# Part of attention's set-up moved behind its first row passes, and more dummy matmuls ahead of the experts

## The chip, the core and the metric

The kernel is one program on one core of a Trainium2 chip. The metric is the device time of one execution, in microseconds, and lower is better.

## The reference

Sliding-window attention with sink tokens, a top-1 mixture of eight experts, and a dense layer pair, one after the other on 1536 tokens:

```
keep = (pos_k < n_sink) | ((pos_q >= pos_k) & (pos_q - pos_k < window))     # 2 batches, 8 heads, 768 tokens, 64 wide
a = exp(where(keep, q @ k.T / 8, -1e9) - rowmax); a /= a.sum + 1e-9
x = (a @ v), heads side by side                                              # 1536 x 512
xn = x / (|x| + 1e-6);  en = expert_emb / (|expert_emb| + 1e-6)
logits = xn @ en.T / tau;  e = argmax;  gate = softmax(logits)[e]
out[t] = gate[t] * (relu(x[t] @ w1[e[t]]) @ w2[e[t]])                        # 512 -> 1024 -> 512
h = out @ w_in;  return max(0.01 * h, h) @ w_out                             # 512 -> 2048 -> 512
```

## The kernel before, in words

Three stages share TensorE. **Attention** runs over 96 items (batch, group of four heads, block of 128 queries, head). An item is a product sc of q with the keys near the block, a row pass on VectorE (line 266: adds a mask of the kind m0, m1, ma, mb or mc, and takes the row's extreme), an exponential on ScalarE (line 268), a transpose of the probabilities and a product with v. Before that, `turns` transposes q and k: TensorE writes tk or tq (line 196), ScalarE copies the high half (lines 202, 216) and VectorE subtracts out the low half, head_k and head_q (lines 207, 217), since float32 products are made of rounded pairs. Blocks 0 to 2 of a group are turned by the functions in the list `first`, blocks 3 to 5 by those in `second`, at steps given by the table SECOND. The masks are made in `setup`, before all this, on VectorE (`penal`, line 116).

**The router** reads each finished block of x. Its set-up (`router_setup`) is a generator of which one piece is issued a step from step 16 on: first the norm of the eight expert embeddings (`norm`, lines 680 to 686, on 8 x 1 elements), their scaling (lines 606 to 608) and transposes, then small tables. At the end of attention a last product rk ranks the tokens, `id_list` makes the list ids of token numbers for each expert by twelve small products (ipa), and GpSimd gathers rows of x by it.

**The experts** follow in a fixed order of widths. Weights come in slots of 512 KB (slot_raw, line 997, on SyncE's DMA queue); ScalarE copies a slot's rounded high half (line 1001) and VectorE subtracts out its low half (line 1002). The first expert here is 128 wide (`moe_narrow`). It uses slots 0 to 7, the second expert slots 8 to 15: TensorE turns the gathered rows (tr), ScalarE and VectorE make mxT of them; then four times twelve products hp with slot 0, 2, 4 or 6, a relu hr on ScalarE (line 1222), two transposes th, the halves h on ScalarE and VectorE (lines 1230, 1231), and six products acc with slot 1, 3, 5 or 7. The second expert's rows become slot_big (line 1073). TensorE's instructions are issued in the order in which the code is written; those of the other engines are ordered by the Tile scheduler, which uses simulated times, and each engine then works through its own list.

`stir(c, n)` issues n matmuls of zeros, 128 x 512, whose result is not read. Two such groups stand around the products ipa, with the counts in WARM: their operand hot is a tile that GpSimd clears after attention. Attention has a group of seven of its own at the program's start, on the tile warm.

Of the kernel before, what the change touches and what calls it, by code (L numbers as in the profile page):

```python
# [7 lines left out]
F32 = mybir.dt.float32  # L8
F32R = mybir.dt.float32r
BF16 = mybir.dt.bfloat16  # L10
# [4 lines left out]
AF = mybir.ActivationFunctionType  # L15
# [6 lines left out]
P = 128  # L22
# [26 lines left out]
MAN = set()  # L49
STIR = {}  # L50
FIRST = [11, 13, 15, 17, 19, 21]
SECOND = [1, 2, 3, 4, 5, 6]
# [29 lines left out]
def setup(c):  # L82
# [37 lines left out]
    nc.vector.tensor_tensor(out=first[:, 1, :], in0=keep[:, P:2 * P], in1=sink[:, 0, :], op=ALU.max)  # L120
    c.m0 = mp.tile([P, P], F32, name="m0")
    penal(c.m0, first[:, 1, :])
    c.m1 = mp.tile([P, 2 * P], F32, name="m1")
    penal(c.m1[:, 0:P], first[:, 0, :])
    penal(c.m1[:, P:2 * P], keep[:, P:2 * P])
    c.ma = mp.tile([P, 2 * P + SINK], F32, name="ma")
    penal(c.ma[:, 0:2 * P], keep)
    penal(c.ma[:, 2 * P:], sink[:, 0, 0:SINK])
    c.mb = mp.tile([P, 2 * P + SINK], F32, name="mb")
    penal(c.mb[:, 0:P], keep[:, 0:P])  # L130
    penal(c.mb[:, P:P + SINK], sink[:, 0, 0:SINK])
    penal(c.mb[:, P + SINK:], keep[:, P:2 * P])
    c.mc = mp.tile([P, 2 * P + SINK], F32, name="mc")
    penal(c.mc[:, 0:SINK], sink[:, 0, 0:SINK])
    penal(c.mc[:, SINK:], keep)
    c.los = cp.tile([P, B * H * QB], F32, name="los")


def attention(c, ctx):
# [45 lines left out]
    def turns(b, pr):  # L185
# [28 lines left out]
        def q_part(c0, j):  # L214
            t, w, qt = turn(rq[:, :, j], c0, f"q{j}"), slice(c0 * P, (c0 + 3) * P), two[j][1]
            nc.scalar.activation(out=qt[:, 0, w], in_=t, func=AF.Copy, scale=-0.125)  # L216
            later(step[0] >= 0, lambda: nc.vector.scalar_tensor_tensor(
                out=qt[:, 1, w], in0=t, scalar=-0.125, in1=qt[:, 0, w].bitcast(F32), op0=ALU.mult, op1=ALU.subtract))

# [11 lines left out]
    load_qk(0, 1, 0, 3)  # L231
    c.warm = att.tile([P, 512], BF16, tag="warm", name="warm", bufs=1)
    nc.vector.memset(c.warm, 0.0)
# [16 lines left out]
    def score(b, g, i, h):  # L250
        if h == 0:
            u = units[b, g, i] = Ctx()
            u.p = wk.tile([P, 4, W3], F32, tag="p", name=f"p{b}{g}{i}", bufs=PB)
            u.pt = {}
        u = units[b, g, i]
        off, n, m, _, s0 = SPAN[i]
        kt, qt = heads[b, 4 * g + h]
        sc = psc.tile([P, W3], F32, tag="sc", name=f"sc{b}{g}{i}{h}")
        w = max(n, 2 * P)
        for half in range(2):  # L260
            nc.tensor.matmul(sc[:, 0:w], lhsT=qt[:, half, i * P:(i + 1) * P], rhs=kt[:, off:off + w],  # L261
                             start=half == 0, stop=half == 1)
        p = u.p[:, h, 0:n]
        col = ((b * 2 + g) * QB + i) * 4 + h
        lo = c.los[:, col:col + 1]
        nc.vector.tensor_tensor_reduce(out=p, in0=sc[:, 0:n], in1=m, scale=1.0, scalar=3.0e38,  # L266
                                       op0=ALU.add, op1=ALU.min, accum_out=lo)
        later(1, lambda: nc.scalar.activation(out=p, in_=p, func=AF.Exp, scale=-1.0, bias=lo))  # L268
        if h == 3 and i >= 2:
            u.sp = wk.tile([P, 4, SINK], F32, tag="sp", name=f"sp{b}{g}{i}")  # L270
            later(2, lambda: nc.gpsimd.tensor_copy(u.sp, u.p[:, :, s0:s0 + SINK]))
# [70 lines left out]
    first, second = group_turns(0, 0)  # L342
    setting = router_setup(c, ctx)
    stir(7)
    n = len(items)
    for _ in range(2):
        first.pop(0)()
    s = 0
    while s < n or after:
# [5 lines left out]
        if s < n:  # L355
# [5 lines left out]
            at = 4 * j + h  # L361
            if s < 3:
                for _ in range(2):
                    if first:
                        first.pop(0)()
            if at in SECOND:
                second.pop(0)()
            if k + 1 < len(groups):
# [11 lines left out]
                if at == 23:  # L380
                    assert not first and not second
                    second = then
            score(b, g, i, h)
        if 0 <= s - LAG1 < n:
            flip(*items[s - LAG1])
        if s >= 16:
            next(setting, None)
        if 0 <= s - LAGS < n and items[s - LAGS][3] == 3 and items[s - LAGS][2] >= 2:
# [204 lines left out]

def router_setup(c, ctx):


# [18 lines left out]

    yield
    c.tri = cp.tile([P, P], BF16, name="tri")
# [13 lines left out]
    c.qsel = table("qsel", NB, 1, -OUT)  # L631
    yield
    c.low = cp.tile([P, E, E], F32, name="lowtri")
# [5 lines left out]
    for n in range(E):  # L639
        nc.gpsimd.memset(c.cb[:, 0, n:n + 1], float(WIDTH[n]))  # L640
        nc.gpsimd.memset(c.cb[:, 1, n:n + 1], float(BASE[n]))
        nc.gpsimd.memset(c.ordv[:, n:n + 1], float(ORDER[n]))
    yield
    c.ss = cp.tile([P, NTT], F32, name="ss")
# [619 lines left out]

WARM = [3, 8]


def stir(c, n):

    if n:  # L1270
        t = c.pacc.tile([P, 512], F32, tag="acc", name=f"stir{c.uid()}")
        for _ in range(n):
            c.nc.tensor.matmul(t, lhsT=c.hot[:, 0:P], rhs=c.hot, start=True, stop=True)

# [187 lines left out]
def program(tc, q, k, v, n_sink, window, emb, tau, w1, w2, w_in, w_out, out):  # L1462
# [11 lines left out]
    with ExitStack() as ctx:  # L1474
# [11 lines left out]
        with tc.manual_schedule(engines={PE}), ExitStack() as mctx:  # L1486
            c.mo = mctx.enter_context(tc.tile_pool(name="m_wk", bufs=1))
            c.conv = [mctx.enter_context(tc.tile_pool(name=f"conv{i}", bufs=1)) for i in range(CONV)]
            c.yT = c.mo.tile([P, 4, YW], F32, name="yT")
            c.hot = c.mo.tile([P, 512], BF16, tag="y", name="hot", bufs=3)  # L1490
            c.nc.gpsimd.memset(c.hot, 0.0)
            for kk in range(4):
# [37 lines left out]
```

## Time and profile before

| what | value |
|---|---|
| median of three runs | 621.79 us (618.84 to 622.26) |
| the profiled execution, its own time | 618.77 us |
| its span, first to last instruction | 617.0 us |
| TensorE matmul busy | 588.9 us, 95% of the span |
| VectorE, ScalarE, GpSimd busy | 396.6, 292.9, 55.1 us |
| mean granted clock of TensorE | 0.971 of full |

The span leaves out 1.8 us around the first and the last instruction. A busy share is an average over stages with different limits, so the stretches of the next sections say more than the table. The granted clock has two levels, 0.50 (1.2 GHz) and 1.00 (2.4 GHz); a value between them is a mean over a stretch.

### The profile page before, as it was taken

How to read it: one execution, taken by the hardware profiler on the slowest of the kernel's cores; microseconds unless marked ns; L12 is line 12 of the kernel's file. 1: busy time of each engine (PE TensorE's matmuls, PEld its weight loads, DVE VectorE, ACT ScalarE, POOL GpSimd, SP SyncE). 2: the span in 40 equal slices, each digit the busy share in tenths (PEclk: the TensorE clock that was granted, in tenths of full speed). 3: DMA queues.
4: the chain of work that ended last, by engine and by line, in shares of the span. 5: the costliest groups of instructions: out<-in, count | busy, mean ns of one | idle time of the engine just before them, and what ended most of it. 6: DMA issues, size and time to landing. Idle time of an engine off the chain costs nothing.

```text
span 617.0 us, 10038 instructions
## 1 busy us (share of the span) xinstructions
PE 588.9 (95%) x3603; PEld 537.8 (87%) x3604; DVE 396.6 (64%) x953; ACT 292.9 (47%) x556; POOL 55.1 (9%) x156
## 2 busy tenths in 40 slices
PE   7899999997699999999999999799999999999996
PEld 4799999895599998889989998698998998899894
DVE  7889788856699659997973799953224322242230
ACT  4777787755687444524652463442223322332230
POOL 3011013003122010001000000010000100020001
PEclk7899999996699999999999999999999999999999
DMA  5777560013998683379499600000000100010001
GB/s 119 172 162 173 144 167 2 2 68 110 346 359 302 196 315 106 119 248 372 157 343 338 240 0 2 0 35 18 1 1 0 52 2 0 1 52 0 1 1 56
DMA packets 87994, 73.71 MB, mean 119 GB/s; under 512 B 54024, under 2 KB 70408, under 8 KB 87936
## 3 DMA queue, kind: packets, MB, share of 16 engines
q1 hardware_dynamic: 85824, 66.22, 34.4%
q0 software_dynamic: 2112, 6.75, 3.1%
q8 instruction: 31, 0.51, 0.4%
q14 instruction: 27, 0.22, 0.1%
HBM read 66.67 MB, written 6.29 MB: 118 GB/s over the span
## 4 chain that ended last, share of the span: by engine, by line
PE 87%; DVE 6%; DMA 2%; issue 2%; ACT 1%; SPq 1%; POOL 0%; POOLq 0%; DVEq 0%
PE acc L1079 30%; PE hp L1079 30%; PE xp L298 6%; PE sc L261 4%; PE hp L1176 3%; PE acc L1188 3%; PE tp L280 3%; DMA slot_raw<-in_moe_w 2%; PE tq L196 1%; PE lg L716 1%; PE xp L301 1%; PE tr L1068 1%; PE xTp L697 1%; PE tk L196 1%; DVE slot L1054 1%
## 5 line engine op out<-in xcount | busy, mean ns | idle before, releaser
L1079 PE MATMUL acc<-slot,h 128*128 128x512 f32 x603 | 151.8, 395 | 4.5 <-DVE slot L1054 3.4
L1079 PE MATMUL hp<-fxT,slot 128*128 128x384 f32 x768 | 142.3, 337 | 0.0
L1079 PEld LDWEIGHTS hp<-fxT,slot 128*128 128x128 f32 x768 | 134.9, 188 | 4.7
L1079 PEld LDWEIGHTS acc<-slot,h 128*128 128x128 f32 x603 | 111.8, 188 | 26.5 <-DVE slot L1054 4.1
L1424 DVE TENSOR_TENSOR lk<-hp,lk 128x384 f32<-128x384 f32 x64 | 35.5, 555 | 101.2 <-ACT lk L1423 101.2
L1423 ACT ACTIVATE lk<-hp 128x384 f32<-128x384 f32 x64 | 31.4, 491 | 126.2 <-PE hp L1079 119.3
L1002 DVE TENSOR_TENSOR slot<-slot_raw,slot 128x1024 fp32r<-128x1024 f32 x48 | 58.3, 1222 | 11.4 <-ACT slot L1001 11.1
L1001 ACT CAST slot<-slot_raw 128x1024 fp32r<-128x1024 f32 x48 | 50.0, 1047 | 18.1 <-DMA slot_raw<-in_moe_w 17.8
L268 ACT ACTIVATE p<-p,los 128x288 f32<-128x288 f32 (+2 forms) x96 | 45.6, 504 | 16.8 <-DVE los L266 16.2
L1079 PE MATMUL acc<-h,slot 128*128 128x256 f32 (+2 forms) x288 | 49.0, 319 | 0.0
L1426 DVE TENSOR_TENSOR h<-lk,h 128x384 fp32r<-128x384 f32 x59 | 32.7, 555 | 24.4 <-ACT h L1425 24.4
L261 PE MATMUL sc<-head_k,head_q 128*128 128x288 f32 (+1 forms) x192 | 43.9, 338 | 3.5 <-DVE head_k L207 1.1
L1079 PEld LDWEIGHTS acc<-h,slot 128*128 128x128 f32 x288 | 43.1, 188 | 2.9
L1425 ACT CAST h<-lk 128x384 fp32r<-128x384 f32 x59 | 30.2, 512 | 31.8 <-DVE lk L1424 31.8
L298 PE MATMUL xp<-v,pt 128*128 128x65 f32 x352 | 43.8, 269 | 0.0
L298 PEld LDWEIGHTS xp<-v,pt 128*128 128x128 f32 x352 | 42.6, 192 | 0.1
L1458 POOL DMA_INDIRECT out_y<-y,sid x12 | 12.4, 1037 | 318.6 <-DVE y L1457 298.4
L261 PEld LDWEIGHTS sc<-head_k,head_q 128*128 128x128 f32 x192 | 29.9, 201 | 6.9 <-ACT head_q L216 3.1
L1079 PE MATMUL hp<-slot_big,slot 128*128 128x256 f32 (+1 forms) x192 | 35.4, 333 | 0.0
L1079 PEld LDWEIGHTS hp<-slot_big,slot 128*128 128x128 f32 x192 | 29.8, 189 | 2.7
L280 PE MATMUL tp<-ident,p 128*128 128x128 f32 x176 | 30.2, 278 | 0.0
L1095 POOL DMA_INDIRECT rows<-xd,ids x16 | 18.6, 1162 | 114.0 <-PE tr L1068 110.7
(252 smaller groups left out, 842.6 us busy)
## 6 DMA issues: line engine op xcount, KB each, us to landing
slot_raw<-in_moe_w SPq DMA_DIRECT2D x56, 512.0 KB
slot_wide<-in_moe_w_in SPq DMA_DIRECT2D x8, 1024.0 KB
slot_wide<-in_moe_w_out SPq DMA_DIRECT2D x8, 1024.0 KB
raw_q<-in_q SPq DMA_DIRECT2D x64, 96.0 KB
slot_first<-in_moe_w SPq DMA_DIRECT2D x8, 512.0 KB
raw_k<-in_k SPq DMA_DIRECT2D x32, 96.0 KB
xd<-x SPq DMA_DIRECT2D x12, 256.0 KB
v<-in_v SPq DMA_DIRECT2D x12, 192.0 KB
```

What stands on the lines that cost most here:

```text
L261: nc.tensor.matmul(sc[:, 0:w], lhsT=qt[:, half, i * P:(i + 1) * P], rhs=kt[:, off:off + w], start=half == 0, stop=half == 1)
L268: later(1, lambda: nc.scalar.activation(out=p, in_=p, func=AF.Exp, scale=-1.0, bias=lo))
L280: nc.tensor.transpose(u.t[:, h % 2, n, :], u.p[:, h, o:o + P], c.ident)
L298: nc.tensor.matmul(xp[:, h, :], lhsT=u.pt[h // 2][:, h % 2, n, :], rhs=vT[b, g][:, kb, h, :], start=h == 0 and n == 0, stop=h == 3 and i < ...
L1001: nc.scalar.copy(out=sl.g[0], in_=sl.raw)
L1002: nc.vector.tensor_tensor(out=sl.g[1], in0=sl.raw, in1=sl.g[0].bitcast(F32), op=ALU.subtract)
L1079: c.nc.tensor.matmul(out, lhsT=a[x], rhs=b[y], start=first and n == 0, stop=last and n == 2)
L1095: c.nc.gpsimd.indirect_dma_start(out=t[0:w], out_offset=None, in_=c.xd[:, :], in_offset=bass.IndirectOffsetOnAxis(ap=c.ids[0:w, q0 + k:q0 ...
L1423: nc.scalar.activation(out=raw, in_=hp, func=AF.Copy, scale=0.01)
L1424: nc.vector.tensor_tensor(out=raw, in0=hp, in1=raw, op=ALU.max)
L1425: x = nc.scalar.copy(out=h[:, 0, :], in_=raw)
L1426: y = nc.vector.tensor_tensor(out=h[:, 1, :], in0=raw, in1=h[:, 0, :].bitcast(F32), op=ALU.subtract)
```

## The change

Five edits. In `setup` only the mask m1 is still made at once; m0, ma, mb and mc are made in `others`, which is called at step 1 behind the row pass just issued. The router's small tables move into `router_tables`, issued ahead of attention's steps; the rest of its set-up (the embeddings' norm, scaling and transposes) starts at step 26, each piece issued behind that step's row pass and exponential. In the first group the functions of `first` are issued three ahead of the steps and then one a step, those of `second` at the positions 3 to 8 rather than 1 to 6. The dummies around ipa are 10 and 28 instead of 3 and 8. Their operand is now warm, cleared at the program's start and kept in the pool of constants; hot and its memset are gone.

```diff
+SETAT = 26
+SECOND0 = [3, 4, 5, 6, 7, 8]
 FIRST = [11, 13, 15, 17, 19, 21]
 SECOND = [1, 2, 3, 4, 5, 6]
...
-    c.m0 = mp.tile([P, P], F32, name="m0")
-    penal(c.m0, first[:, 1, :])
     c.m1 = mp.tile([P, 2 * P], F32, name="m1")
     penal(c.m1[:, 0:P], first[:, 0, :])
     penal(c.m1[:, P:2 * P], keep[:, P:2 * P])
-    c.ma = mp.tile([P, 2 * P + SINK], F32, name="ma")
-    penal(c.ma[:, 0:2 * P], keep)
...
+    def others():
+        penal(c.ma[:, 0:2 * P], keep)
+        penal(c.ma[:, 2 * P:], sink[:, 0, 0:SINK])
+        penal(c.mb[:, 0:P], keep[:, 0:P])
...
-    c.warm = att.tile([P, 512], BF16, tag="warm", name="warm", bufs=1)
+    c.warm = c.const.tile([P, 512], BF16, name="warm")
...
-    setting = router_setup(c, ctx)
+    router_tables(c)
+    setting = router_setup(c)
     stir(7)
     n = len(items)
-    for _ in range(2):
+    for _ in range(3):
         first.pop(0)()
...
-            if s < 3:
-                for _ in range(2):
-                    if first:
-                        first.pop(0)()
-            if at in SECOND:
+            if s < 3 and first:
+                first.pop(0)()
+            if at in (SECOND if k else SECOND0):
                 second.pop(0)()
...
             score(b, g, i, h)
+            if s == 1:
+                with tc.issue_after(c.scored.ins):
+                    c.others()
...
-        if s >= 16:
-            next(setting, None)
+        if s >= SETAT:
+            with tc.issue_after(c.scored.ins), tc.issue_after(c.raised.ins):
+                next(setting, None)
...
-WARM = [3, 8]
+WARM = [10, 28]
...
-            c.nc.tensor.matmul(t, lhsT=c.hot[:, 0:P], rhs=c.hot, start=True, stop=True)
+            c.nc.tensor.matmul(t, lhsT=c.warm[:, 0:P], rhs=c.warm, start=True, stop=True)
...
-            c.hot = c.mo.tile([P, 512], BF16, tag="y", name="hot", bufs=3)
-            c.nc.gpsimd.memset(c.hot, 0.0)
```

What the scheduler makes of it shows in the engines' lists. First VectorE at the eighth item of attention, where blocks 3 to 5 of the first pair of heads come in. Before:

```order
L684 TENSOR_TENSOR nq_e<-nq_e,ss 8x1
L685 TENSOR_TENSOR ny_e<-nq_e,ny_e 8x1
L207 TENSOR_TENSOR head_k_134<-tk_324,head_k_134 64x384
L207 TENSOR_TENSOR head_k_136<-tk_324,head_k_136 64x384
L686 TENSOR_SCALAR ny_e<-ny_e 8x1
L217 SCALAR_TENSOR_TENSOR head_q_135<-tq_339,head_q_135 128x384
L606 TENSOR_SCALAR ny_e<-ny_e,tau 8x1
L607 RECIPROCAL ny_e<-ny_e 8x1
L217 SCALAR_TENSOR_TENSOR head_q_137<-tq_350,head_q_137 128x384
L608 TENSOR_SCALAR emb<-emb,ny_e 8x512
```

And now, from the eighth row pass on:

```order
L274 ISA p_440,los<-sc_495,ma 128x288
L274 ISA los 128x1
L211 TENSOR_TENSOR head_k_134<-tk_422,head_k_134 64x384
L211 TENSOR_TENSOR head_k_136<-tk_422,head_k_136 64x384
L223 SCALAR_TENSOR_TENSOR head_q_135<-tq_435,head_q_135 128x384
L223 SCALAR_TENSOR_TENSOR head_q_137<-tq_447,head_q_137 128x384
```

The norm's operations (nq_e, ny_e, emb) have left this place; they now stand one by one between row passes of the second group.

Second, ScalarE where the first expert begins. The tiles slot_67, 71, 75, 79, 83, 87, 91, 95 are slots 0 to 7 in the order of loading. Before:

```order
L1001 CAST slot_71<-slot_raw_72 128x1024
L1072 CAST mxT_2569<-tr_2581 128x512
L1001 CAST slot_75<-slot_raw_76 128x1024
L1001 CAST slot_79<-slot_raw_80 128x1024
L1001 CAST slot_83<-slot_raw_84 128x1024
L1222 ACTIVATE hr_2606<-hp_2592 128x256
L1001 CAST slot_87<-slot_raw_88 128x1024
L1230 CAST h_2611<-th_2608 128x256
L1001 CAST slot_91<-slot_raw_92 128x1024
L1222 ACTIVATE hr_2630<-hp_2616 128x256
```

And now:

```order
L1017 CAST slot_71<-slot_raw_72 128x1024
L1017 CAST slot_75<-slot_raw_76 128x1024
L1017 CAST slot_79<-slot_raw_80 128x1024
L1088 CAST mxT_2574<-tr_2606 128x512
L1017 CAST slot_83<-slot_raw_84 128x1024
L1017 CAST slot_87<-slot_raw_88 128x1024
L1017 CAST slot_91<-slot_raw_92 128x1024
L1238 ACTIVATE hr_2631<-hp_2617 128x256
L1017 CAST slot_95<-slot_raw_96 128x1024
L1246 CAST h_2636<-th_2633 128x256
```

The copies of slots 2 and 3 have moved ahead of mxT, and those of slots 5 and 6 ahead of the first hr.

Third, VectorE in the same pass, up to the low half of the second expert's second block of rows (the second slot_big; slot_99, 103, 107, 111, 115 and 119 are slots 8 to 13). Before:

```order
L1231 TENSOR_TENSOR h_2611<-th_2608,h_2611 128x256
L1002 TENSOR_TENSOR slot_91<-slot_raw_92,slot_91 128x1024
L1002 TENSOR_TENSOR slot_95<-slot_raw_96,slot_95 128x1024
L1231 TENSOR_TENSOR h_2653<-th_2650,h_2653 128x256
L1073 TENSOR_TENSOR slot_big<-tr_2658,slot_big 128x4x128
L1002 TENSOR_TENSOR slot_99<-slot_raw_100,slot_99 128x1024
L1002 TENSOR_TENSOR slot_103<-slot_raw_104,slot_103 128x1024
L1231 TENSOR_TENSOR h_2691<-th_2688,h_2691 128x256
L1073 TENSOR_TENSOR slot_big<-tr_2696,slot_big 128x4x128
```

And now:

```order
L1018 TENSOR_TENSOR slot_95<-slot_raw_96,slot_95 128x1024
L1247 TENSOR_TENSOR h_2636<-th_2633,h_2636 128x256
L1018 TENSOR_TENSOR slot_99<-slot_raw_100,slot_99 128x1024
L1018 TENSOR_TENSOR slot_103<-slot_raw_104,slot_103 128x1024
L1018 TENSOR_TENSOR slot_107<-slot_raw_108,slot_107 128x1024
L1247 TENSOR_TENSOR h_2678<-th_2675,h_2678 128x256
L1089 TENSOR_TENSOR slot_big<-tr_2683,slot_big 128x4x128
L1018 TENSOR_TENSOR slot_111<-slot_raw_112,slot_111 128x1024
L1018 TENSOR_TENSOR slot_115<-slot_raw_116,slot_115 128x1024
L1247 TENSOR_TENSOR h_2716<-th_2713,h_2716 128x256
L1018 TENSOR_TENSOR slot_119<-slot_raw_120,slot_119 128x1024
L1089 TENSOR_TENSOR slot_big<-tr_2721,slot_big 128x4x128
```

The subtractions of slots 10 to 13 now stand ahead of the second slot_big, where slot 9 was the last before. From the second expert's middle on the lists of all engines agree again.

## Rows read from the trace of the kernel before

**Rows 1.** The page: span, and TensorE's busy time (share of the span) and instructions.

```profile
span 617.0 us, 10038 instructions
...
PE 588.9 (95%) x3603; PEld 537.8 (87%) x3604; DVE 396.6 (64%) x953; ACT 292.9 (47%) x556; POOL 55.1 (9%) x156
```

**Rows 2.** Stretches: length, busy time (instructions) by engine, granted clock, DMA share, GB/s.

```profile
0.00:25.00 25.00, 18.48 (x71) 12.72 (x72) 20.36 (x88) 14.12 (x30) 5.39 (x66) 0.73 0.65 144
25.00:141.00 116.00, 115.00 (x973) 111.31 (x971) 93.27 (x374) 85.19 (x205) 14.90 (x57) 1.00 0.43 103
154.00:158.00 4.00, 0.72 (x2) 0.00 (x0) 2.20 (x2) 2.71 (x3) 1.35 (x2) 0.93 0.93 280
158.00:168.00 10.00, 7.42 (x31) 6.50 (x32) 6.09 (x7) 6.07 (x8) 0.95 (x1) 0.50 1.04 366
168.00:180.00 12.00, 12.00 (x80) 10.78 (x80) 11.37 (x14) 10.73 (x18) 4.11 (x3) 0.99 1.07 365
180.00:300.00 120.00, 120.00 (x801) 112.54 (x800) 101.07 (x178) 63.40 (x94) 10.43 (x9) 1.00 0.70 235
```

**Rows 3.** Timeline of TensorE, 144 to 182 us: start, length, instruction, [idle before <-releaser].

```profile
146.50 0.17 PE L733 MATMUL rk<-cum,ones 128*128 128x16 bf16 x1
149.60 0.61 PE L1273 MATMUL stir<-hot 128*128 128x512 bf16 x1 [2.93 <-POOL hot L1491]
...
151.22 3.50 PE L1273 MATMUL stir<-hot 128*128 128x512 bf16 x8
158.74 1.11 PE L1068 MATMUL tr<-ident,rows 128*128 128x128 f32 x4 [4.02 <-DMA rows<-xd,ids]
160.53 3.23 PE L1079 MATMUL hp<-slot,mxT 128*128 128x256 f32 x12 [0.68 <-ACT mxT L1072]
...
165.27 2.91 PE L1079 MATMUL hp<-slot,mxT 128*128 128x256 f32 x12
...
170.04 1.65 PE L1079 MATMUL hp<-slot,mxT 128*128 128x256 f32 x12
...
176.52 1.67 PE L1079 MATMUL hp<-slot_big,slot 128*128 128x256 f32 x12
```

**Rows 4.** Timeline of ScalarE, 148 to 182 us (slots 4 and 6, and hr).

```profile
163.55 1.04 ACT L1001 CAST slot<-slot_raw 128x1024 fp32r<-128x1024 f32 x1 [1.18 <-DMA slot_raw<-in_moe_w]
164.50 0.38 ACT L1222 ACTIVATE hr<-hp 128x256 f32<-128x256 f32 x1
...
167.05 1.05 ACT L1001 CAST slot<-slot_raw 128x1024 fp32r<-128x1024 f32 x1 [0.81 <-DMA slot_raw<-in_moe_w]
```

**Rows 5.** Timeline of VectorE, 5 to 26 us: a mask, the norm's first, a low half.

```profile
6.90 0.28 DVE L116 TENSOR_SCALAR ma<-keep 128x256 f32<-128x256 f32 x1
...
16.93 0.14 DVE L680 TENSOR_SCALAR ny_e<-ss 8x1 int32<-8x1 int32 x1
...
19.27 1.14 DVE L207 TENSOR_TENSOR head_k<-tk,head_k 64x384 fp32r<-64x384 f32 x2
```

**Rows 6.** Waits of TensorE, 17 to 23 us: us in total, times, longest.

```profile
PE sc L261 <- DVE head_k L207: 1.1, 1, 1.1
PE sc L261 <- DVE head_q L217: 0.6, 1, 0.6
PE tq L196 <- DMA raw_q<-in_q: 0.2, 1, 0.2
```

**Rows 7.** Timeline of VectorE, 158 to 182 us (slots 6 to 9, h, second slot_big).

```profile
168.13 1.22 DVE L1002 TENSOR_TENSOR slot<-slot_raw,slot 128x1024 fp32r<-128x1024 f32 x1 [0.56 <-ACT slot L1001]
169.58 1.22 DVE L1002 TENSOR_TENSOR slot<-slot_raw,slot 128x1024 fp32r<-128x1024 f32 x1 [0.22 <-ACT slot L1001]
170.72 0.42 DVE L1231 TENSOR_TENSOR h<-th,h 128x256 fp32r<-128x256 f32 x1
...
171.93 2.44 DVE L1002 TENSOR_TENSOR slot<-slot_raw,slot 128x1024 fp32r<-128x1024 f32 x2 [0.20 <-ACT slot L1001]
...
174.63 0.68 DVE L1073 TENSOR_TENSOR slot_big<-tr,slot_big 128x512 fp32r<-128x512 f32 x1
```

More of the change, by code (lines that the diff above doesn't have):

```diff
@@ L125, in setup @@
     penal(c.m1[:, P:2 * P], keep[:, P:2 * P])
-    c.ma = mp.tile([P, 2 * P + SINK], F32, name="ma")
-    penal(c.ma[:, 0:2 * P], keep)
[L128 to L135, printed above, removed]
+    c.m0 = mp.tile([P, P], F32, name="m0")
+    c.ma, c.mb, c.mc = (mp.tile([P, 2 * P + SINK], F32, name=nm) for nm in ("ma", "mb", "mc"))
+    def others():
+        penal(c.ma[:, 0:2 * P], keep)
+        penal(c.ma[:, 2 * P:], sink[:, 0, 0:SINK])
+        penal(c.mb[:, 0:P], keep[:, 0:P])
+        penal(c.mb[:, P:P + SINK], sink[:, 0, 0:SINK])
+        penal(c.mb[:, P + SINK:], keep[:, P:2 * P])
+        penal(c.mc[:, 0:SINK], sink[:, 0, 0:SINK])
+        penal(c.mc[:, SINK:], keep)
+        penal(c.m0, first[:, 1, :])
+    c.others = others
     c.los = cp.tile([P, B * H * QB], F32, name="los")
@@ L216, in q_part, with rest @@
             nc.scalar.activation(out=qt[:, 0, w], in_=t, func=AF.Copy, scale=-0.125)
-            later(step[0] >= 0, lambda: nc.vector.scalar_tensor_tensor(
-                out=qt[:, 1, w], in0=t, scalar=-0.125, in1=qt[:, 0, w].bitcast(F32), op0=ALU.mult, op1=ALU.subtract))
+            def rest():
+                c.low_half = nc.vector.scalar_tensor_tensor(out=qt[:, 1, w], in0=t, scalar=-0.125, in1=qt[:, 0, w].bitcast(F32),
+                                                            op0=ALU.mult, op1=ALU.subtract)
+            later(step[0] >= 0, rest)
         for j in range(2):
@@ L265, in score, with raised @@
         lo = c.los[:, col:col + 1]
-        nc.vector.tensor_tensor_reduce(out=p, in0=sc[:, 0:n], in1=m, scale=1.0, scalar=3.0e38,
-                                       op0=ALU.add, op1=ALU.min, accum_out=lo)
-        later(1, lambda: nc.scalar.activation(out=p, in_=p, func=AF.Exp, scale=-1.0, bias=lo))
+        c.scored = nc.vector.tensor_tensor_reduce(out=p, in0=sc[:, 0:n], in1=m, scale=1.0, scalar=3.0e38,
+                                                  op0=ALU.add, op1=ALU.min, accum_out=lo)
+        def raised():
+            c.raised = nc.scalar.activation(out=p, in_=p, func=AF.Exp, scale=-1.0, bias=lo)
+        later(1, raised)
         if h == 3 and i >= 2:
@@ L591, in general, with router_setup @@
                 nc.sync.dma_start(out=c.out[(b * QB + i) * P:(b * QB + i + 1) * P, :], in_=y[:, b * QB + j])
-def router_setup(c, ctx):
+def router_setup(c):
     nc, tc = c.nc, c.tc
@@ L614, in router_setup, with router_tables @@
     nc.vector.tensor_copy(c.embT, t)
-    yield
+def router_tables(c):
+    nc = c.nc
+    cp = c.const
     c.tri = cp.tile([P, P], BF16, name="tri")
@@ L631, in router_setup @@
     c.qsel = table("qsel", NB, 1, -OUT)
-    yield
     c.low = cp.tile([P, E, E], F32, name="lowtri")
@@ L642, in router_setup @@
         nc.gpsimd.memset(c.ordv[:, n:n + 1], float(ORDER[n]))
-    yield
     c.ss = cp.tile([P, NTT], F32, name="ss")
```

## Prediction

> **What bounds the kernel now.** I read the page first for the shares: TensorE is busy for 588.9 of 617.0 us [rows 1], so time can only be won where it waits or runs slowly. The stretches show where that is [rows 2]. From 25 to 141 us it is busy for 115.0 of 116 us at the full granted clock, from 180 to 300 us for all of it, so nothing is to be won there, and whatever arrives late at 180 us stays late. The two weak places are the first 25 us (18.48 us busy, mean clock 0.73) and the passage from attention into the experts: from 158 to 168 us the granted clock is 0.50, the lower level of 1.2 GHz, and TensorE is busy for 7.42 of 10 us. From 168 to 180 us VectorE is nearly full too: 11.37 of 12 us. The change touches just these two places.
>
> TensorE's timeline of the passage [rows 3]: the dummies wait until 149.60 for the memset of their operand (2.93 us of idle time), eight more run from 151.22 for 3.50 us, 0.44 each, and end at 154.7. Then it idles 4.02 us for the gathered rows, until 158.74. The clock of 154 to 158 us is 0.93, so the grant came up about when the dummies ended and was gone when the rows arrived. The first twelve products (hp) take 3.23 us, the next twelve 2.91, the same twelve 1.65 at the full clock from 170.04. The second expert begins at 176.52.
>
> Who releases these products? ScalarE's timeline [rows 4]: the copy of slot 4 starts at 163.55 when its DMA lands, and hr, which TensorE's next transpose reads, starts behind it at 164.50. The copy of slot 6 starts at 167.05, its wait again ended by a DMA. I compared this with ScalarE's queue as the program issues it: the trace runs it in exactly that order. So the first pass of the experts is paced by the landing of weights, through what stands ahead of hr in ScalarE's queue.
>
> **The change, part by part.** I cost it on the profiled execution: 618.77 us, the span and 1.77 around it. The median of the runs shown is 621.79, 3.0 us more, so this execution is near the fast end, and I carry differences over to the median.
>
> *The front.* In the old order VectorE spends 16.93 to 19.27 us on thirteen small operations of the embeddings' norm, 0.18 apart, and only then starts head_k's low half, for which TensorE waits 1.1 us [rows 5, 6]. Its next wait, 0.6 us on head_q's low half, falls where the other norm operations lie. Removing them saves at most these 1.7 us directly; the transposes of blocks 3 to 5 still wait for raw_q to land (0.2 us) [rows 6], in a queue of loads that the change doesn't reorder there. I take 1.2, with 0 and 2.5 as the ends: 0 if the landings take over, 2.5 if the few us behind it at a low clock shorten as well (the first 25 us have 6.5 us of TensorE idle). The eight mask operations that go behind the first scores take at most 0.28 us each [rows 5], together no more than 2.2; they leave the way of the first pair's head_k and come back on VectorE ahead of the second pair's. What is next on TensorE, block 3's transposes, waits for raw_q either way, so I take 0. If that cover were gone, it is up to 2.2 us, for or against.
>
> *The norm's new place.* Seventeen operations at 0.18 us are 3.1 us of VectorE, now between the row passes of the second group. From 25 to 141 us VectorE has 116 - 93.27 = 22.7 us free [rows 2], so most is covered; TensorE is full there, hence a delay is lost if it shows. Between 0 and 3.1 I take 0.2. Loading the third eid on SyncE ahead of slot 2's loads, and the few memsets moved on GpSimd, lie beside transfers already under way: 0.
>
> *The ten dummies.* They no longer wait for the memset, so they can start when VectorE has read the last rank product (rk, at 146.50 [rows 3]), at about 147.0. At 0.44 us they end at 151.4, against 150.9 for the three of before: the index list, the gather and the loads from slot 2 on are 0.5 us later at 1.2 GHz, 0 at 2.4. These loads queue behind slots 0 and 1, which are still moving, so I take 0.1.
>
> *The twenty-eight.* The grant came up some 5 us after the dummies began; from 147.0 that is 152, so most run at 0.22 us and end at about 158, just ahead of the rows. All 28 at 0.44 would end at 164. Either way the first hr, below, comes later still, so this costs nothing by itself: 0.
>
> *The order behind them.* This is where I expect the change to be decided, and it is not in the diff: the scheduler has moved the copies and subtractions of later slots ahead of the row passes. In the new queue of ScalarE the copies of slots 2 and 3 stand ahead of mxT, and those of 4, 5 and 6 ahead of the first hr. Slot 6 lands at 167.05 [rows 4], its copy ends at 168.10, so the first hr can't start before 168.1 instead of 164.50: 3.6 us of TensorE standing still, whatever its clock was. On VectorE the low half of the second expert's rows (slot_big, at 174.63 [rows 7]) has subtractions 0 to 13 ahead of it instead of 0 to 9. Four at 1.22 us are 4.9 us [rows 7]; the gaps of VectorE in that stretch take back 0.56 + 0.22 + 0.20 = 1.0, so 3.9 is the lower end. Followed from hr: 168.1 + 0.4, copy of slot 7 until 169.5, its subtraction until 170.8, h until 171.2; then three subtractions, h, a slot_big, two subtractions, h, one more and the second slot_big: 6 x 1.22 + 2 x 0.42 + 2 x 0.68 = 9.5, that is 180.7 without a gap, 4.2 after 176.52. Copies 8 to 14 still wait for landings and for hr, up to 1.7 us of gaps more, so 5.9 is the upper end. I take 4.5, since the queue sums, which need no guess on landings, are near the low end. From there TensorE is full to 300 us, and the subtractions done early save it nothing.
>
> A clock that is kept would not help here: with hp at 1.65 instead of 3.23 us its result would lie ready even longer while hr waits. By the Trainium skill ("TensorE: Matmul & The Clock Gate", section "Terms") throttled time times one half is the penalty; for the 10 us at 0.50 that is an estimate of 5 us to win, and the sum by it would be -6. The rows speak against it, since at 163.55 and 167.05 a DMA ends the wait and no matmul does; it stands as a rival.
>
> **Sum:** -1.2 + 0.2 + 0.1 + 4.5 = +3.6. This execution would take 622.4, the median **625.4 us**.
>
> **Rivals.**
> - *The clock decides (faster).* If the grant holds from 158.74 on and the copies of slots 4 to 6 come early enough, the two hp shrink by 1.6 and 1.3 us and the first tr by half of its 1.11: -3.4 [rows 3]. With the front's 1.2 that is -4.6: 617.2. For it: 10 us at half clock. Against it: the DMA rows at 163.55 and 167.05. It decides if slot 6 lands before about 163.5.
> - *The front gives more (about the same).* All 2.5 us, and 2 more from a clock that rises earlier: a mean of 0.73 over 25 us is some 13.5 us at half speed, of which 4 spared give 2. -4.5 + 0.3 + 4.5 = +0.3: 622.1. For it: VectorE is at 20.36 of 25 us there [rows 2]; against it, raw_q's landing.
> - *More is lost (slower still).* The norm's 3.1 us show in the full stretch, or the landings add their 1.4: +6.5 to +8, 628 to 630. It needs VectorE to be late for scores where TensorE has 1.0 us of idle in 116.
>
> **How the numbers follow.** A difference below 0.5% (3.1 us) can hardly be told from none in this kernel. The forecast gets 0.57, with a range of its own of 622.5 to 628.5 (order 3.9 to 5.9, front 0 to 2.5 and the runs' own spread of 3 us); about two thirds of that lies above +3.1. The clock gets 0.17, the greater front 0.16, more loss 0.10. Faster: 0.17 and 0.03 of the greater front, 0.20. Slower: 0.36 and 0.09, 0.45. Same: 0.35. Leaving out the faster part of the clock's case and the end of the last, the range is 618.5 to 628.5.
>
> **What would show it.** Counted from attention's last rank product (146.50 before), the copy of slot 6 should still begin 20 to 21 us later, now with hr straight behind it and TensorE idle ahead of the first th, and the second expert's first hp 34 to 36 us later instead of 30.0. The first 25 us should show head_k's second low half about 1.2 us earlier. The dummies should start about 0.5 us behind the rank product, with the grant at 1.00 about 5 us on. I am wrong if th begins near 165 (slot 6's copy is not what hr waits for), if the rank product comes over 2.5 us earlier, or if attention ends later than before.

## Result and the profile after

The changed kernel takes 625.46 us (median of seven runs, 625.19 to 628.66) against 621.85 for before (seven runs, 618.84 to 623.13); the ratio is 1.0084, 95% interval [1.0061, 1.0107], about 5 us slower by that ratio, while the two medians lie 3.6 us apart. A second measurement on another chip gave 626.40 against 620.28, 1.0102 [1.0072, 1.0133]. The forecast of 625.4 lies on the first median, but two of its terms were wrong, as the profile shows; its profiled execution took 625.46.

The page after, the span and TensorE's busy time, answers to [rows 1]. TensorE is busy for 8.9 us more, 27 further dummies among it, and the span is 6.6 us longer: a larger busy share is no gain here.

```profile
span 623.6 us, 10102 instructions
PE 597.8 (96%) x3631; PEld 542.4 (87%) x3631; DVE 396.8 (64%) x953; ACT 293.1 (47%) x556; POOL 54.1 (9%) x155
```

The stretches after, with the columns of [rows 2] (length, busy time by engine, granted clock, DMA share, GB/s):

```profile
0.00:25.00 25.00, 21.37 (x93) 15.36 (x94) 19.34 (x73) 14.54 (x29) 5.53 (x66) 1.00 0.65 145
25.00:141.00 116.00, 113.11 (x935) 109.26 (x935) 94.14 (x386) 85.09 (x205) 14.97 (x57) 0.99 0.44 103
158.00:168.00 10.00, 5.33 (x23) 3.56 (x21) 6.39 (x7) 5.03 (x6) 1.28 (x2) 0.77 1.01 343
168.00:180.00 12.00, 9.84 (x57) 8.83 (x58) 10.08 (x11) 9.92 (x15) 1.31 (x2) 0.76 1.07 366
180.00:300.00 120.00, 120.00 (x796) 111.73 (x795) 96.87 (x176) 59.50 (x90) 12.92 (x11) 1.00 0.71 236
```

In the first 25 us TensorE is busy for 2.9 us more. The clock of 1.00 in that row is not what was granted. TensorE's timeline has these two groups of three transposes there:

```profile
9.24 0.84 PE L200 MATMUL tk<-ident,raw_k 128*128 128x128 f32 x3
20.12 0.49 PE L200 MATMUL tk<-ident,raw_k 128*128 128x128 f32 x3
```

In the trace of before three such transposes take 0.84 us at 9.60 us, where the granted clock is 0.50. So here the clock was 0.50 up to about 20 us: the view counts the time ahead of the first recorded change of the clock as full, and the means of these first microseconds (0.73 before, 1.00 after) can't be compared. The stretch that was full before, 25 to 141, has lost 1.9 us of TensorE's work. From 158 to 168 the clock is better (0.77 for 0.50) and TensorE does less.

TensorE's timeline of the passage after, which answers to [rows 3]:

```profile
148.09 0.17 PE L749 MATMUL rk<-cum,ones 128*128 128x16 bf16 x1
148.61 4.43 PE L1289 MATMUL stir<-warm 128*128 128x512 bf16 x10 [0.35 <-DVE sel L752]
153.20 6.20 PE L1289 MATMUL stir<-warm 128*128 128x512 bf16 x28
160.68 0.63 PE L1084 MATMUL tr<-ident,rows 128*128 128x128 f32 x4 [1.28 <-issue]
163.48 0.80 PE L1095 MATMUL hp<-slot,mxT 128*128 128x256 f32 x2 [2.18 <-ACT mxT L1088]
170.11 0.69 PE L1244 MATMUL th<-ident,hr 128*128 128x128 f32 x2 [2.75 <-ACT hr L1238]
182.15 1.88 PE L1095 MATMUL hp<-slot_big,slot 128*128 128x256 f32 x12
```

And ScalarE's, as [rows 4]:

```profile
165.40 2.23 ACT L1017 CAST slot<-slot_raw 128x1024 fp32r<-128x1024 f32 x2 [1.97 <-DMA slot_raw<-in_moe_w]
168.73 1.04 ACT L1017 CAST slot<-slot_raw 128x1024 fp32r<-128x1024 f32 x1 [1.10 <-DMA slot_raw<-in_moe_w]
169.68 0.38 ACT L1238 ACTIVATE hr<-hp 128x256 f32<-128x256 f32 x1
```

The last rank product stands at 148.09 instead of 146.50. Slot 6's copy begins 20.6 us behind it, when its DMA lands, hr comes straight behind the copy, and TensorE stands still for 2.75 us ahead of th. From the rank product to the second expert it is 34.06 us instead of 30.02. From there to the end it is 441.4 instead of 440.5 (the two spans less 182.15 and 176.52). So the 6.6 us by which the two spans differ are 1.6 in attention, 4.0 in the passage and 1.0 behind it.

Attention is ahead of before until 45 us (its 29th row pass starts at 44.55 instead of 46.45) and behind from 60 us on (its 49th at 76.19 instead of 74.33). What lies between shows in TensorE's timeline at 50 to 55 us, in the second group:

```profile
50.04 1.08 PE L310 MATMUL xp<-v,pt 128*128 128x65 f32 x8 [0.41 <-DVE x L324]
52.25 1.08 PE L310 MATMUL xp<-v,pt 128*128 128x65 f32 x8 [1.13 <-DMA raw_q<-in_q]
53.26 0.41 PE L626 MATMUL embT_ps<-ident,emb 8*128 8x8 f32 x4
53.60 0.55 PE L200 MATMUL tq<-ident,raw_q 128*128 128x128 f32 x3
53.98 1.70 PE L292 MATMUL tp<-ident,p 128*128 128x128 f32 x8
```

VectorE's timeline there, some of the norm's operations and what ends the waits:

```profile
51.45 0.12 DVE L701 TENSOR_TENSOR ny_e<-nq_e,ny_e 8x1 f32<-8x1 f32 x1
51.57 0.42 DVE L324 TENSOR_TENSOR x<-xp,rec 128x256 f32<-128x256 f32 x1
52.50 0.47 DVE L622 TENSOR_SCALAR emb<-emb,ny_e 8x512 f32<-8x512 f32 x1
53.70 0.19 DVE L628 COPY embT<-embT_ps 128x32 f32<-128x32 f32 x1 [0.73 <-PE embT_ps L626]
```

embT, the turned embeddings, stands in TensorE's list ahead of the transposes tp of eight probability blocks, and it can't start before the norm's last operation ends at 52.97. The second xp starts 0.26 us behind the end of x (51.99), which reads what the xp before it wrote; the DMA that its row names is a last semaphore, not what it lacked, I take it. This list also shows a mistake of mine in the section on the kernel: TensorE's instructions are issued in the order of the code in the experts only. In attention the scheduler orders TensorE as well.

### The profile page after: what moved, and what is told of

It is laid out like the page before. It is cut to its first block, busy times and chain, and to the rows that moved or that the text cites. A ratio compares the mean times of both kernels' runs of the same rounds, so it can differ in the third digit from the quotient of the medians.

```text
span 623.6 us, 10102 instructions
## 1 busy us (share of the span) xinstructions
PE 597.8 (96%) x3631; PEld 542.4 (87%) x3631; DVE 396.8 (64%) x953; ACT 293.1 (47%) x556; POOL 54.1 (9%) x155
## 4 chain that ended last, share of the span: by engine, by line
PE 83%; DVE 7%; DMA 3%; issue 3%; ACT 2%; SPq 1%; POOL 0%; POOLq 0%; DVEq 0%; ACTq 0%
PE hp L1095 29%; PE acc L1095 29%; PE xp L310 5%; PE sc L269 4%; PE tp L292 3%; PE tq L200 2%; DMA slot_raw<-in_moe_w 2%; PE hp L1192 2%; PE acc L1204 2%; PE lg L732 1%; PE xp L313 1%; PE tk L200 1%; DMA raw_q<-in_q 1%; PE xTp L713 1%; PE tr L1084 1%
## 5 line engine op out<-in xcount | busy, mean ns | idle before, releaser
L1017 ACT CAST slot<-slot_raw 128x1024 fp32r<-128x1024 f32 x48 | 50.1, 1047 | 21.5 <-DMA slot_raw<-in_moe_w 21.3
L269 PE MATMUL sc<-head_k,head_q 128*128 128x288 f32 (+1 forms) x192 | 45.9, 345 | 1.6 <-DVE head_k L211 1.0
L1441 ACT CAST h<-lk 128x384 fp32r<-128x384 f32 x59 | 30.2, 512 | 31.8 <-DVE lk L1440 31.7
```

What stands on the lines that cost most here:

```text
L1017: nc.scalar.copy(out=sl.g[0], in_=sl.raw)
L1441: x = nc.scalar.copy(out=h[:, 0, :], in_=raw)
```

## The experiments

Every kernel was timed beside the kernel before on its chip (medians there 620.06, 620.28 and 621.01). Passage is the time from the last rank product to the second expert's first hp.

| run | median, us | ratio to before, 95% interval | last rk at | passage |
|---|---|---|---|---|
| front_only | 624.12 | 1.0061 [1.0038, 1.0083] | 147.01 | 32.0 |
| warm_only | 624.08 | 1.0052 [1.0030, 1.0074] | 147.22 | 34.1 |
| held | 623.09 | 1.0045 [1.0026, 1.0064] | 146.94 | 31.2 |
| emb_late | 624.48 | 1.0072 [1.0048, 1.0096] | 145.42 | 34.8 |
| early_before | 619.78 | 0.9981 [0.9967, 0.9996] | 147.37 | 29.3 |
| early_all | 621.25 | 1.0021 [0.9994, 1.0049] | 149.62 | 29.5 |
| norm_back | 623.01 | 1.0045 [1.0028, 1.0062] | 145.37 | 33.6 |
| changed_again | 626.40 | 1.0102 [1.0072, 1.0133] | 148.20 | 33.9 |
| best_38 | 620.37 | 0.9996 [0.9977, 1.0015] | 145.27 | 30.0 |
| best_11 | 618.53 | 0.9966 [0.9950, 0.9983] | 145.22 | 29.3 |
| pops_only | 618.56 | 0.9956 [0.9929, 0.9983] | 145.68 | 30.0 |
| masks_only | 624.12 | 1.0049 [1.0028, 1.0069] | 149.18 | 31.8 |

**The two halves.** front_only is the changed kernel with `WARM = [3, 8]` on hot and its memset, and with warm in attention's pool again; warm_only is the kernel before with warm in the pool of constants, without hot and its memset, and with

```diff
-WARM = [3, 8]
+WARM = [10, 28]
...
-            c.nc.tensor.matmul(t, lhsT=c.hot[:, 0:P], rhs=c.hot, start=True, stop=True)
+            c.nc.tensor.matmul(t, lhsT=c.warm[:, 0:P], rhs=c.warm, start=True, stop=True)
```

> The changed kernel with the dummies of before (3 and 8, on hot, with its memset). In the changed kernel the last rank product ends 1.6 us later than before (148.09 against 146.50) and from it to the second expert's first hp are 34.1 us against 30.0. Theory, two separate losses: attention keeps its own, so the last rank product stands at 147.5 to 148.5; the passage is mostly that of before, since the copies 0 to 3 stand around mxT as before and only slot 5's copy has moved ahead of the first hr: 30.5 to 32. The time is 2 to 3.5 us above before. Rival, the dummies are the whole loss and the front is a gain: last rank product at 145 to 145.5, the time 1 us below before.

> The kernel before with the dummies alone changed (10 and 28 on warm, no memset). Its list for ScalarE has the copies 0 to 6 ahead of the first hr, as in the changed kernel, but only slots 7 and 8 ahead of the second expert's first rows. Theory, the order behind the dummies: the last rank product stays at 146.5 within 0.4, the first hr starts straight behind slot 6's copy, 21 to 22 us behind the rank product (18.0 before, 21.6 in the changed kernel), and the second expert's first hp comes 32.5 to 34.1 us behind it; the time is 2.5 to 4 us above before. Rival, more dummies keep the clock and win: hp at 1.65 us, the passage at 28 to 30, the time the same or lower.

TensorE's timeline in front_only, from the last rank product to the second expert:

```profile
147.01 0.17 PE L749 MATMUL rk<-cum,ones 128*128 128x16 bf16 x1
166.68 0.44 PE L1244 MATMUL th<-ident,hr 128*128 128x128 f32 x2 [2.61 <-ACT hr L1238]
179.00 1.67 PE L1095 MATMUL hp<-slot_big,slot 128*128 128x256 f32 x12
```

And in warm_only:

```profile
147.22 0.18 PE L733 MATMUL rk<-cum,ones 128*128 128x16 bf16 x1
168.76 0.69 PE L1228 MATMUL th<-ident,hr 128*128 128x128 f32 x2 [2.42 <-ACT hr L1222]
181.36 1.68 PE L1079 MATMUL hp<-slot_big,slot 128*128 128x256 f32 x12
```

The dummies alone bring the whole loss of the passage, with th 21.5 us behind the rank product. Their rival, a kept clock that wins, is out. The front alone loses too. Its rank product is 0.5 later, less than the 1.0 to 2.0 expected, and its passage is 2.0 longer, since slot 5's copy has moved ahead of hr. Behind the passage its profile takes 444.7 us for 440.5; two waits of TensorE for ScalarE, 0.8 and 0.7 us, are part of that, and a fall of the clock at 406 us, of which more in the last section. Each half is some 3 to 4 us slower, the whole 5 to 6. In the passage the losses overlap (2.0 and 4.1 us alone, 4.0 together); for the times the intervals are too wide to say so.

The rank product of warm_only missed its expectation (147.22 for 146.5 within 0.4), although the lists of TensorE, VectorE and ScalarE in its attention are those of before. early_before, below, has the same lists and 147.37. So the 146.50 of before is an early execution, and a difference from it of up to 0.9 us in attention can be one between executions.

**The order repaired.** held is the changed kernel in which slots' copies are issued as the first expert needs them, which is ScalarE's order of before up to the second h (slot 8's copy then still stands ahead of the first slot_big):

```diff
-    c.work.pop(Q0)
+    c.work.pop(2)
...
+    c.work.pop(3, c.high)
...
+        if c.lead:
+            c.work.pop(1, r)
...
-        c.work.pop(QN, x, y)
+        c.work.pop(6 if c.lead and i == 3 else QN, x, y)
```

(high is mxT's copy, r is hr, lead is true in the first expert.)

> The changed kernel with the copies of slots 2 to 4 held behind mxT and those from slot 5 on released one by one behind hr and h, which gives ScalarE and VectorE the order of before in the first expert. Theory: the first hr starts behind slot 4's copy, 17.5 to 18.5 us behind the last rank product instead of 21.6, the passage falls from 34.1 to 30 to 31 us, and the time is 3 to 4 us below the changed kernel, 1 to 2.5 above before; the last rank product stays at 148.1. Rival, the landing of the weights paces the second expert anyway, so work done earlier only waits elsewhere: the passage stays above 33 us and the time within 1 us of the changed kernel.

ScalarE's timeline of held, slots 4 and 5:

```profile
164.86 1.04 ACT L1017 CAST slot<-slot_raw 128x1024 fp32r<-128x1024 f32 x1 [2.17 <-DMA slot_raw<-in_moe_w]
165.81 0.38 ACT L1238 ACTIVATE hr<-hp 128x256 f32<-128x256 f32 x1
166.73 1.05 ACT L1017 CAST slot<-slot_raw 128x1024 fp32r<-128x1024 f32 x1 [0.53 <-DMA slot_raw<-in_moe_w]
```

Now hr stands behind slot 4's copy, 18.9 us behind the rank product instead of 21.6 (0.4 above the expectation, for slot 4 landed later), and 2.8 of the passage's 4.0 us are back. By the ratios it is 0.39 to 0.57% below the changed kernel's two measurements, 2.4 to 3.5 us, at or below the lower end of the 3 to 4 expected, and still 2.8 above before rather than 1 to 2.5. Its rank product came at 146.94, not at 148.1, for a reason that the next part shows. early_before goes one step further on the kernel before: slot 4's copy stands behind the first hr, too (`pop(2, c.high)`, and `pop((2, 1, 1, 6)[i] if c.lead else QN, x, y)`).

> The kernel before with one copy moved: slot 4's now stands behind the first hr on ScalarE (and its subtraction behind the first h's path on VectorE), slots 5 and 6 behind the first h; all else as before. Theory, hr waits for the copies queued ahead of it and so for landings: the first hr starts when its products end, 17.2 to 17.6 us behind the last rank product instead of 18.0, the first th 0.4 to 0.8 us earlier, and the second expert's first hp 28.5 to 29.8 instead of 30.0; the time 0.3 to 1.5 us below before. Rival, the landings pace the expert whatever the order: slots 6 and 8 are needed next, the second expert stays at 30.0 within 0.3 and the time is the same.

TensorE's timeline of early_before, the first th and the second expert:

```profile
165.09 0.69 PE L1230 MATMUL th<-ident,hr 128*128 128x128 f32 x2 [0.47 <-ACT hr L1222]
176.69 1.68 PE L1079 MATMUL hp<-slot_big,slot 128*128 128x256 f32 x12
```

TensorE's wait ahead of th is 0.47 us; th comes 17.7 us behind the rank product and the passage takes 29.3. This alone beats the kernel before. The Trainium skill ("PSUM — Partial Sum Buffer", section "Engine vs sequencer instructions") says that the queues of ScalarE, VectorE and GpSimd are strictly first in, first out; these three positions of hr agree.

**The norm's place.** emb_late puts embT seven steps later (`for _ in range(8): yield` ahead of its transposes); norm_back issues the norm from step 16 without the two orderings, which puts it in the front again.

> The changed kernel with seven more empty steps between the norm's last operation and the four transposes embT on TensorE. In the changed kernel TensorE idles about 1.5 us at 50 to 54 us, with embT queued ahead of three transposes of probabilities, and its clock is 0.50 from 54.2 to 57.6. Theory, TensorE's order costs this: with embT late the transposes come first again, the idle time there falls below 0.5 us, the clock stays at 1.00, the last rank product stands at 144.5 to 146, and the time is 2 to 3.5 us below the changed kernel. Rival, VectorE's time for the norm costs it: the same 17 operations still lie between the row passes, the last rank product stays at 147.5 or later, and the time stays within 1 us.

> The changed kernel with the norm issued from step 16 again and without the two orderings, so that it stands in the front as before; masks, first and second pops and dummies stay changed. Theory, the norm's new place costs attention 1.9 us (the row passes go from 1.8 us ahead to 0.1 behind between items 28 and 40) and gave the front part of its 1.8: here the front gains 0.5 to 1.5, nothing is lost behind it, the last rank product stands at 145 to 146, and the passage is 33.5 to 34.2 us as with the dummies alone; the time 2 to 3.5 us above before. Rival, the norm in the front was what the 1.8 us came from: the last rank product at 146.3 or later and the time 4 us above before.

> The changed kernel once more, on the chip of these runs. Theory: the idle 1.5 us of TensorE at 50 to 54 us stays, and whether the clock then falls to 0.50 for 3.4 us differs from execution to execution, so that the last rank product stands at 146.9 to 147.1 without the fall and 148.1 with it (or up to 1.7 later still where the front is slow); the passage is 33.8 to 34.3 us each time. Rival, the fall belongs to the idle time and comes each time: 148.1 again.

The stretch of 48 to 58 us, columns as in [rows 2]. Before, with the ten microseconds from 44 us on ahead of it:

```profile
44.00:54.00 10.00, 10.00 (x85) 9.70 (x85) 8.57 (x30) 7.97 (x20) 1.06 (x7) 1.00 0.74 167
48.00:58.00 10.00, 9.55 (x80) 8.95 (x79) 8.97 (x30) 8.29 (x19) 2.02 (x12) 1.00 0.74 167
```

The changed kernel:

```profile
48.00:58.00 10.00, 8.46 (x57) 7.86 (x55) 6.98 (x34) 4.68 (x10) 1.12 (x7) 0.83 0.60 135
```

held, whose attention is that of the changed kernel:

```profile
48.00:58.00 10.00, 8.46 (x72) 7.89 (x70) 8.22 (x37) 5.53 (x12) 1.25 (x8) 1.00 0.62 140
```

emb_late:

```profile
48.00:58.00 10.00, 8.55 (x72) 7.96 (x70) 9.87 (x50) 7.44 (x16) 1.74 (x11) 1.00 0.63 141
```

norm_back:

```profile
48.00:58.00 10.00, 9.55 (x82) 9.06 (x80) 9.74 (x35) 8.70 (x21) 2.03 (x12) 1.00 0.80 181
```

changed_again:

```profile
48.00:58.00 10.00, 8.46 (x56) 7.87 (x55) 6.98 (x34) 4.58 (x10) 1.13 (x7) 0.83 0.59 133
```

With the norm here TensorE idles for 1.5 us, with it in the front for 0.45. My theory on embT's place fell: with embT late the idle time is still 1.45 us, and VectorE is full (9.87 of 10); TensorE's waits there, 0.8 us for emb and 0.7 for a row pass, both end with VectorE. The rank product of emb_late is early (145.42) as expected, but not for the reason given, and its passage and what follows took 1.2 of these 2.7 us back; by the ratios its time is 0.7 to 1.9 us below the changed kernel, not 2 to 3.5. The run with the norm back in the front is the clean answer: 145.37, and the passage of the dummies' order (33.6). It shows that the norm's place costs this. How it does is not settled: in the changed kernel VectorE is busy for only 6.98 of these ten microseconds (8.22 in held), and the longest idle piece stands where TensorE's own list, ordered anew by the scheduler, has two xp next to each other with x on VectorE between them; in emb_late VectorE is full. In the changed kernel a fall of the clock comes on top: 0.83 is a mean with 0.50 for about 3.4 us. It fell in both profiles of the changed kernel and in neither of front_only and held, whose attention is the same; their rank products stand 1.1 to 1.3 us earlier. For changed_again that is between its two theories: 148.2 as the rival said, but the fall doesn't belong to this attention each time. The Trainium skill ("TensorE: Matmul & The Clock Gate", section "What's actually happening") says that the number of slow matmuls at a kernel's start varies from run to run with the phase of the clock's gate. These four profiles, two with a fall and two without, are in line with such a difference between executions, in the middle of a kernel, where that sentence says nothing.

**Both repairs, and what the dummies are worth.** early_all is emb_late with the copies of early_before; best_38 is norm_back with them; best_11 is best_38 with the dummies of before.

> The changed kernel with both repairs: embT seven steps later, and the copies of the first expert's slots issued behind mxT, hr and h as in the run on the kernel before (slot 4 behind the first hr). Theory: the last rank product at 144.5 to 145.5, the first hr 17.3 to 18 us behind it, the second expert 29 to 31 us behind it, that is at 174 to 176 against 176.5 before and 182.2 changed; the time 0 to 2 us below before, 5 us below the changed kernel. Rival, an earlier attention only waits for the loads behind the index list: the second expert 31.5 us or more behind the rank product, and the time 1 to 3 us above before.

> The changed kernel with the norm back in the front and the order of the first expert repaired (slot 4's copy behind the first hr): 10 and 28 dummies on warm. Theory, both losses gone and the gain of the second blocks' new place kept: the last rank product at 145.0 to 145.8, the second expert 29.2 to 30 us behind it, the time 1 to 3 us below before. Rival, an earlier attention doesn't shorten the passage's wait for weights: 31 us or more, the time that of before.

> The same with the dummies of before (3 and 8 on hot). Theory, the dummies are worth nothing in themselves, since hr's wait and the landings of weights set the passage: the second expert within 0.4 us of the run with 10 and 28, counted from the last rank product, and the time within 1 us of it. Rival, 28 dummies keep the clock up for the first products: here the passage is longer by 1 us or more.

The stretch of 58 to 66 us in early_all:

```profile
58.00:66.00 8.00, 8.00 (x44) 7.92 (x43) 2.25 (x7) 2.79 (x7) 0.29 (x1) 0.57 0.98 206
```

early_all's passage is 29.5 as expected, but its profiled rank product stands at 149.62: the clock was at 0.50 for nearly all of this stretch, right behind the norm's. That missed its expectation, and its runs spread from 618.14 to 626.37. best_11 is 2 us faster than before. best_38, with 27 dummies more, takes the time of before, which only its rival expected, though its passage is 30.0 and not 31. So both theories on the dummies missed: without them the passage is 0.7 us shorter and the time 1.8 us lower. TensorE's waits in best_38 from 172 to 345 us (us in total, times, longest):

```profile
PE ty L1272 <- ACT y L1265: 1.6, 1, 1.6
PE tr L1083 <- DVE slot_big L1088: 0.3, 1, 0.3
```

TensorE's timeline of best_38, the first expert's first products:

```profile
159.20 0.50 PE L1094 MATMUL hp<-slot,mxT 128*128 128x256 f32 x2 [0.68 <-ACT mxT L1087]
159.93 2.50 PE L1094 MATMUL hp<-slot,mxT 128*128 128x256 f32 x10 [0.23 <-DVE mxT L1088]
```

The same products in best_11:

```profile
159.02 3.23 PE L1094 MATMUL hp<-slot,mxT 128*128 128x256 f32 x12 [0.68 <-ACT mxT L1087]
```

Twelve products take 3.23 us either way (162.43 - 159.20). The dummies win nothing here, and best_38 has two waits that best_11 lacks, 1.9 us together; in its lists the copy of slot 8 stands ahead of the first slot_big copy and that of slot 10 ahead of the second. That this order makes the two waits is argued from these rows, not tried by itself. Behind the passage the profile of best_38 takes 444.7 us and that of best_11 441.1. The rest of these 3.6 us, 1.7, is no cost of the dummies that is shown: it goes with a fall of the clock to 0.50 for 3.4 us in the profiled execution of best_38. The stretch of 400 to 408 us, first best_38, then best_11:

```profile
400.00:408.00 8.00, 6.34 (x24) 5.50 (x25) 5.37 (x7) 2.20 (x5) 0.00 (x0) 0.79 0.00 0
400.00:408.00 8.00, 8.00 (x40) 6.83 (x39) 5.47 (x11) 4.01 (x8) 0.00 (x0) 1.00 0.00 0
```

**The front's parts.** Each is the kernel before with one edit.

> The kernel before with only the new places of the functions in first and second in the first group (three ahead, then one a step; positions 3 to 8). Theory, these give most of the front's gain that the norm's removal was credited with: the last rank product at 145.2 to 146.0 and items 20 to 44 of the row passes 0.7 to 1.3 us ahead of before, as with the norm back in the front; the experts' order is that of before, the time 0 to 1.5 us below before. Rival, the masks give it: the last rank product stays at 146.3 to 147.4.

> The kernel before with only the masks m0, ma, mb and mc made behind the first row passes. Theory, they are hidden: row passes and last rank product within 0.5 us of before (up to 1.3 later where the clock falls at 20 to 27 us, as in two other runs of that attention); but the list of ScalarE now has slot 5's copy ahead of the first hr, so the passage is 31.5 to 32.3 us and the time 1 to 2 us above before. Rival, the masks give the front's gain: the last rank product at 145.2 to 146.0.

The last rank product in TensorE's timeline of pops_only:

```profile
145.68 0.17 PE L732 MATMUL rk<-cum,ones 128*128 128x16 bf16 x1
```

And of masks_only:

```profile
149.18 0.17 PE L738 MATMUL rk<-cum,ones 128*128 128x16 bf16 x1
```

The new places of first and second make the gain: 0.8 us against the early 146.50 of before, 1.5 to 1.7 against the two other profiles of that attention (147.22 and 147.37), and 2.7 us of time by the ratio, more than the 1.5 expected. The masks alone have the passage that was expected (slot 5's copy ahead of hr), but lose 2.7 us of attention (1.8 to 2.0 against the two other profiles), against my expectation. Most of the loss shows behind the front: the 25th row pass in VectorE's timeline is 0.2 us later than before's, the 45th 3.2. Its cause stays open. One rival is that execution's clock: three transposes take 0.84 to 0.85 us there at 20.27 and 23.80 us and 0.49 only at 27.98, while in before they take 0.49 at 20.18 already, 0.84 to 0.85 at 22.38 and 23.87, and 0.49 again at 28.13. In the full change (norm_back) the masks do no such harm, so the parts don't add up.

## Why the prediction came out right, and where it was wrong

- **The order behind the dummies (+4.5; measured +4.0).** Right, with its mechanism: slot 6's copy 20.6 us behind the rank product (20 to 21 forecast), hr straight behind, the second expert at 34.06 (34 to 36). warm_only gives the same with the dummies alone, held and early_before move hr and get the time back. That mxT would be late too (its hp 15.4 us behind the rank product instead of 14.0) I had not priced; it is covered by hr's wait.
- **The ten dummies (+0.1).** ipa comes 4.74 us behind the rank product instead of 4.35. Small, as forecast.
- **The twenty-eight (0).** They ended at 159.4, 11.3 us behind the rank product, as forecast (11.5), ahead of the rows. As a cause of a new order they cost, once the rest is repaired, 1.9 us (best_38 less best_11); a term that I had left out.
- **The front (-1.2).** The size was about right: the 29th row pass starts 1.9 us earlier (44.55 for 46.45). The cause was not: with the norm still in the front 1.1 of it are there (norm_back), most of it from the new places of first and second (pops_only), which I had not priced. The sign that I named for it came out small: head_k's second low half starts 0.5 us earlier (18.79 for 19.27), not 1.2, since VectorE now waits 1.45 us there for ScalarE's copy. The clock is not the reason for the lead either: in emb_late, with 0.67 from 13 to 20 us and 0.77 to 25, the 29th row pass starts at 44.09.
- **The norm's new place (+0.2; measured, behind the 29th row pass, about +2 without a fall of the clock, over 3 with one).** This step failed. "VectorE has 22.7 us free [rows 2], so most is covered" took the mean of 116 us; in the ten where most of the operations land (44.1 to 53.0 us in the changed kernel) VectorE had 1.0 to 1.4 us free in before (8.97 of 10 from 48 us on, 8.57 from 44 on). norm_back shows the cost; that too little cover is its mechanism is argued, beside TensorE's new order there. The upper end, 3.1, holds the first value and not the second. "Attention ends later than before" was on my list of what would make me wrong, and it does.
- **The sum.** On the profiled executions it is +6.6, not +3.6: attention +1.6 for -1.0 (up to 0.9 of the 1.6 can be the early execution of before), passage +4.0 for +4.6, the rest +1.0 for 0. Of the 1.0 it stays open how much is the change: from the second expert on, early_before takes 441.3 us and pops_only 441.1, and their experts differ little from before's (440.5) or not at all. That 625.4 met the median is partly luck: before's profiled execution is its fastest, that of the changed kernel is not, and I carried +3.6 from the one to the median of all; the first measurement's medians happen to differ by 3.6, and by the ratios the change costs 5 to 6 us.
- **The rivals.** The clock did not decide: in 158 to 168 it was 0.77 for 0.50 and TensorE waited for hr. "The front gives more" asked for up to 2.5 us and a clock that rises earlier; the lead was 1.9, with the clock at 0.50 up to about 20 us, and attention lost it again. The 13.5 us at half speed in that rival were too few: the mean of 0.73 counts the first 4 us as full, though the seven dummies there take 3.17 us, 0.45 each. "More is lost", by the norm's 3.1 us in the full stretch, is what joined the forecast.

## What to carry to other kernels

Read an added or moved instruction's cover from the ten microseconds where it lands, not from a long stretch's mean, and look at the order of the engine that waits for it. Test a granted clock at the start of a trace by the length of equal instructions: 1.00 stood there for 20 us at half speed. Where a scheduler orders the queues, compare the lists ahead of every wait that a transfer ends: the copies ahead of one small operation cost 3 to 4 us here, and moving a single one behind it gained about 1. An edit's parts, measured alone, don't add up when each deals the lists anew; the two best versions here keep the new places of first and second, and the first expert's order of before (pops_only) or one held by hand (best_11). pops_only with early_before's order was not tried.

## What the runs showed that I had not expected

In three of the six profiles with the norm in its new place (changed, changed_again, early_all) the clock fell to 0.50 behind that stretch, in the middle of attention, for 3.4 to 6.8 us; what TensorE did before it was 8.5 us of work in 10, with idle pieces of 1.1 us and less. front_only and held did the same work there and kept the clock. In four profiles (front_only, held, best_38 and early_all) the clock also fell for 3.4 us between 402 and 410 us; held's stretch behind the passage is 443.1 us where the changed kernel, without that fall, has 441.4 and 441.3. So a profile's sum can hold some 1.7 us of such a fall, which need not come from the change. Seventeen operations on VectorE, all but one on 8 x 1 elements and of 0.12 to 0.20 us, cost TensorE over 1 us of idle time (1.5 for 0.45), in a stage where VectorE is busy for 80% on the mean.
